# Where a mixture-of-experts stage issues its row gathers and weight fetches: ahead of a block's first layer, or behind it

## The chip, the cores and the metric

The kernel runs on one core of one Trainium2 chip. The metric is the device time of one execution in microseconds (us). The kernel before takes 1376.26 us as the median of 3 runs (1374.75 to 1378.42).

## What is computed

Three stages follow one another on 4608 tokens of width 512. Attention with keys and values pooled by eight gives `x`; a dense feed-forward layer with softplus replaces it; then comes the expert stage, which is where the change lies:

```
skip_score = x @ w_skip
do_compute = skip_score > 0
xc = x[do_compute]
logits = xc @ w_gate
e_idx = argmax(logits); gate_w = softmax(logits)[e_idx]
for e in range(8):
    h = max(xc[e_idx == e] @ w1[e], 0)
    y[e_idx == e] = gate_w * (h @ w2[e])
out[do_compute] = xc + y          (all other rows: out = x)
```

## The kernel before, in words

**Blocks.** The expert stage sorts the tokens by expert into blocks of up to 256 tokens (two halves, j = 0 and 1, of 128). A program of conditional blocks covers the worst case; block `i` is written by `superblock(i, ...)`. Blocks 0 to 9 form the first part (`NS1 = 10`), whose lists are made before the last group of tokens of the dense layer is ready; blocks 10 to 26 form the second part, nested in one another by conditions. Of these 27, the profiled execution runs 20, blocks 0 to 19; blocks past 19 are called dead here. Nothing is computed for a dead block, but a running block still issues the loads for the blocks that follow it, dead or not.

**One block.** TensorE (PE) does layer one in 96 matmuls (128x256, L898) into four PSUM tiles `h`. ScalarE (ACT) evicts each as `hh` (L902), VectorE (DVE) as the remainder `hl` (L903). Layer two is 24 matmuls (128x512, L922 to L924) for each half into `y`; DVE adds the residual (`ys`, L926) and GpSimd (POOL) scatters each half to `out` (L928). The second half is skipped when the block holds too few tokens.

**Loads, all issued by POOL on one queue.** `load_ids` (L349) fetches a block's row numbers, `gather` (L357) its rows by these numbers into `xg` (two DMAs, four buffers), `fetch` (L396) the weights of an expert into `raw1` (first layer) or `raw2` (second layer), one buffer of 2 MiB each. If a block has the same expert as the one before it, the fetch carries indices out of bounds and moves nothing. The list for `load_ids` of a dead block is out of bounds too, so a gather for one uses row numbers that an earlier block left.

**Weights into place.** When the expert changes, `split1` turns `raw1` into `w1h` (ACT, L405, four pieces) and `w1l` (DVE, L406, four pieces) behind layer one of the block before, under a condition (L911). `split2` does the same for the second layer (L413, L414) at the head of the block itself (L883).

**Rows into place.** `spread(i + 2)` at the head of block `i` transposes 32x32 pieces of `xg` on DVE (L380) and issues 16 DMAs on SyncE (SP, L385); `turn(i + 1)` in the middle of layer one writes the operands of the next block (L391, L392).

**What sets the order.** This stage is under a manual schedule: each engine runs its instructions in the order in which they are written. POOL's order in a block before the change is fetch `raw1` of the next block, gather for the block three ahead, row numbers for the block four ahead, fetch `raw2` of the next block, and then the two scatters:

```
            if more > 0:
                fetch("raw1", w1, i + 1)
            ...
            if more > 2:
                gather(i + 3)
            if more > 3:
                load_ids(i + 4)
            if i > 0 and i != NS1 - 1:
                with tc.If(changes(s)):
                    split2()
            if more > 0:
                fetch("raw2", w2, i + 1)
```

Of the kernel before, what the change touches and what calls it, by code (L numbers as in the profile page):

```python
# [36 lines left out]
def tile_kernel(ctx, tc, qT, kT, vT, wbits, w9, w1, w2, out):  # L37
# [7 lines left out]
    NS1 = 10  # L45
# [298 lines left out]
    def at(i):  # L344
        return (lists[1], i) if i < NS1 else (lists[2], i - NS1)

    def load_ids(i):
        li, s = at(i)
        nc.gpsimd.indirect_dma_start(  # L349
            out=ids[i % 5], out_offset=None, in_=tab,  # L350
            in_offset=bass.IndirectOffsetOnAxis(ap=li["tidx"][:, s:s + 1], axis=0),
            bounds_check=P * NCOL // 2 - 1, oob_is_err=False)

    def gather(i):
        rows = NTOK - G if i < NS1 else NTOK
        for j in range(2):
            nc.gpsimd.indirect_dma_start(  # L357
                out=xg[i % 4][j], out_offset=None, in_=x2d[:rows, :],
                in_offset=bass.IndirectOffsetOnAxis(ap=ids[i % 5][:, j:j + 1], axis=0),
                bounds_check=rows - 1, oob_is_err=False)  # L360
# [26 lines left out]
    def turn(i):  # L387
        xv = xm[i % 2].rearrange("p (q k j r) -> p j q k r", q=4, k=4, j=2)
        hv, lv = (t.rearrange("p k (j q r) -> p j q k r", j=2, q=4) for t in (xth[i % 2], xtl[i % 2]))
        for j in range(2):  # L390
            nc.scalar.activation(out=hv[:, j], in_=xv[:, j], func=AF.Copy)  # L391
            nc.vector.tensor_tensor(out=lv[:, j], in0=xv[:, j], in1=hv[:, j].bitcast(F32), op=ALU.subtract)  # L392

    def fetch(name, src, i):
        li, s = at(i)
        nc.gpsimd.indirect_dma_start(  # L396
            out=ws[name], out_offset=None, in_=src,
            in_offset=bass.IndirectOffsetOnAxis(ap=li["widx"][:, s:s + 1], axis=0),
            bounds_check=NE * P - 1, oob_is_err=False)

    def split1():
        raw = ws["raw1"].rearrange("p (a b) -> p a b", a=4)
        for q in range(4):
            cs = slice(q * 256, (q + 1) * 256)
            nc.scalar.activation(out=ws["w1h"][:, :, cs], in_=raw[:, :, cs], func=AF.Copy)  # L405
            nc.vector.tensor_tensor(out=ws["w1l"][:, :, cs], in0=raw[:, :, cs],  # L406
                                    in1=ws["w1h"][:, :, cs].bitcast(F32), op=ALU.subtract)

    def split2():
        raw = ws["raw2"].rearrange("p (a b) -> p a b", a=8)  # L410
        for q in range(4):
            cs = slice(q * 2, (q + 1) * 2)
            nc.scalar.activation(out=ws["w2h"][:, cs, :], in_=raw[:, cs, :], func=AF.Copy)  # L413
            nc.vector.tensor_tensor(out=ws["w2l"][:, cs, :], in0=raw[:, cs, :],  # L414
                                    in1=ws["w2h"][:, cs, :].bitcast(F32), op=ALU.subtract)
# [447 lines left out]
    def superblock(i, cond, mask, more, big=None):  # L863

        _, s = at(i)

        def changes(s_):
            return (mask & (1 << s_)) > 0

        with ExitStack() as st:  # L870
            if cond is not None:
                st.enter_context(tc.If(cond))
            if more > 0:
                fetch("raw1", w1, i + 1)
            if i == 0 and more > 0:
                gather(1)
                gather(2)
            if more > 2:
                gather(i + 3)
            if more > 3:  # L880
                load_ids(i + 4)
            if i > 0 and i != NS1 - 1:
                with tc.If(changes(s)):  # L883
                    split2()
            if more > 0:
                fetch("raw2", w2, i + 1)
            if more > 1 and i not in (0, NS1):
                spread(i + 2)
            xh, xl = xth[i % 2], xtl[i % 2]
            for fp in range(4):  # L890
                h = ps_f.tile([P, 2, SB], F32, tag="h", name="h")
                for f2 in range(2):
                    f0 = (fp * 2 + f2) * P
                    n = 0
                    for kk in range(4):
                        wh, wl = ws["w1h"][:, kk, f0:f0 + P], ws["w1l"][:, kk, f0:f0 + P]
                        for l, r in ((wh, xh), (wh, xl), (wl, xh)):
                            nc.tensor.matmul(h[:, f2, :], lhsT=l, rhs=r[:, kk, :],  # L898
                                             start=n == 0, stop=n == 11)
                            n += 1  # L900
                fs = slice(fp * 2, fp * 2 + 2)
                nc.scalar.activation(out=hh[:, fs, :], in_=h, func=AF.Relu)  # L902
                nc.vector.scalar_tensor_tensor(out=hl[:, fs, :], in0=h, scalar=0.0,  # L903
                                               in1=hh[:, fs, :].bitcast(F32),
                                               op0=ALU.max, op1=ALU.subtract)
                if fp == 1 and i > 0 and more > 0:
                    turn(i + 1)
            if more > 0:
                if i == 0:
                    flip(1, ps_t, "t")  # L910
                with tc.If(changes(s + 1)):  # L911
                    split1()
            if more > 1 and i in (0, NS1):
                spread(i + 2)
            for j in range(2):
                with ExitStack() as half:  # L916
                    if j and big is not None:
                        half.enter_context(tc.If((big & (32 << s)) > 0))
                    y = ps_o.tile([P, D], F32, tag=f"y{j}", name=f"y{j}")
                    js = slice(j * P, (j + 1) * P)  # L920
                    for f in range(8):
                        nc.tensor.matmul(y, lhsT=hh[:, f, js], rhs=ws["w2h"][:, f, :], start=f == 0, stop=False)  # L922
                        nc.tensor.matmul(y, lhsT=hh[:, f, js], rhs=ws["w2l"][:, f, :], start=False, stop=False)  # L923
                        nc.tensor.matmul(y, lhsT=hl[:, f, js], rhs=ws["w2h"][:, f, :], start=False, stop=f == 7)  # L924
                    r = xg[i % 4][j]
                    nc.vector.scalar_tensor_tensor(out=ys[j], in0=y, scalar=r[:, D:D + 1],  # L926
                                                   in1=r[:, :D], op0=ALU.mult, op1=ALU.add)
                nc.gpsimd.indirect_dma_start(  # L928
                    out=out, out_offset=bass.IndirectOffsetOnAxis(ap=ids[i % 5][:, j:j + 1], axis=0),
                    in_=ys[j], in_offset=None, bounds_check=NTOK - 1, oob_is_err=False)  # L930
# [84 lines left out]
```

## Time and profile before

| | |
|---|---|
| median of 3 runs | 1376.26 us (1374.75 to 1378.42) |
| time of the profiled execution | 1372.43 us |
| its span, first to last instruction | 1370.6 us |
| mean granted TensorE clock | 0.995 of full speed |
| PE busy | 1336.9 us, 98% of the span |
| DVE, ACT, POOL busy | 847.9, 594.5, 309.5 us |

The span leaves out 1.8 us of the profiled execution's own time, at its start and end. The expert stage's first layer-one matmul starts at 909.6 us, so the stage takes about 460 us. A time such as "1316.40" below is counted from the span's start. An engine is busy while it executes an instruction; the idle time ahead of an instruction is given in brackets with the event that ended it.

### The profile page before, as it was taken

The page shows a single profiled execution, that of the slowest core. Times are in us where ns is not written, and L with a number is a line of the kernel's source. Part 1 is how long each engine was busy: PE and PEld are TensorE (multiplying, and loading weights), DVE is VectorE, ACT ScalarE, POOL GpSimd, SP SyncE. Part 2 cuts the span into 40 slices and gives each one's busy share as a digit, 9 for nine tenths or more (in the row PEclk, how much of TensorE's full clock was granted, in tenths as well). Part 3 has the DMA queues.
Part 4 walks back from the last instruction along what each step waited for, and adds up shares of the span by engine and source line. Part 5 has one row for each costly group of instructions (what it writes and reads, how often), then busy time and mean ns, then how long its engine had stood idle before and what let it go on. Part 6 is the DMA issues. An engine that isn't in the chain of part 4 may idle for free. (4 is left out here: it accounts for less than half of the span.)

```text
span 1370.6 us, 21360 instructions
## 1 busy us (share of the span) xinstructions
PE 1336.9 (98%) x7030; PEld 1113.8 (81%) x7030; DVE 847.9 (62%) x1951; ACT 594.5 (43%) x1076; POOL 309.5 (23%) x374
## 2 busy tenths in 40 slices
PE   6999999999999999999999999999999999999986
PEld 5777887878878778778778878888989998889886
DVE  7997884974974965956947839534645432325254
ACT  6995554545445545545445445541111111114142
POOL 2010111121121030020120210342424243323332
PEclk9999999999999999999999999999999999999998
DMA  8643442241341340431411302513323122225272
GB/s 276 250 148 86 116 109 63 79 126 32 97 114 34 109 119 7 127 96 41 125 43 48 95 9 58 182 47 86 96 68 108 57 76 66 76 62 169 64 275 76
DMA packets 149600, 134.18 MB, mean 98 GB/s; under 512 B 100789, under 2 KB 116789, under 8 KB 146912
## 3 DMA queue, kind: packets, MB, share of 16 engines
q1 hardware_dynamic: 131744, 95.51, 24.1%
q0 software_dynamic: 17728, 37.13, 8.5%
q8 instruction: 60, 0.98, 0.3%
q14 instruction: 68, 0.56, 0.1%
HBM read 166.67 MB, written 29.67 MB: 143 GB/s over the span
## 5 line engine op out<-in xcount | busy, mean ns | idle before, releaser
L716 PE MATMUL h<-xh,wt 128*128 128x512 f32 x1152 | 379.6, 390 | 0.3 <-DVE xl L573 0.3
L716 PEld LDWEIGHTS h<-xh,wt 128*128 128x128 f32 x1152 | 216.2, 188 | 46.0 <-DVE xl L573 1.2
L898 PE MATMUL h<-xt,w1h 128*128 128x256 f32 x1280 | 229.2, 282 | 6.2 <-issue 2.8
L740 PE MATMUL y<-wt,gh 128*128 128x512 f32 x576 | 232.8, 404 | 0.0
L120 DVE CUSTOM_DVE_ANT_0 junk<-rows,w9b 128x512 bf16<-128x512 f32 x324 | 223.1, 689 | 8.1 <-ACT rows L114 3.2
L741 PE MATMUL y<-wt,gh 128*128 128x512 f32 x576 | 225.2, 391 | 0.0
L742 PE MATMUL y<-wt,gl 128*128 128x512 f32 x576 | 225.1, 391 | 0.0
L716 PE MATMUL h<-xl,wt 128*128 128x512 f32 x576 | 224.7, 390 | 0.0
L898 PEld LDWEIGHTS h<-xt,w1h 128*128 128x128 f32 x1280 | 197.9, 189 | 10.2 <-issue 5.6
L898 PE MATMUL h<-xt,w1l 128*128 128x256 f32 x640 | 180.3, 282 | 1.9 <-DVE w1l L406 0.8
L902 ACT ACTIVATE hs<-h 128x512 fp32r<-128x512 f32 x80 | 47.5, 597 | 310.5 <-PE h L898 159.2
L725 DVE SCALAR_TENSOR_TENSOR a<-h,a 128x512 f32<-128x512 f32 x144 | 98.8, 686 | 103.3 <-ACT a L724 102.5
L722 ACT ACTIVATE a<-h 128x512 f32<-128x512 f32 x144 | 85.8, 596 | 174.1 <-PE h L716 162.3
L727 ACT ACTIVATE gh<-a 128x512 fp32r<-128x512 f32 x144 | 91.0, 632 | 161.5 <-DVE a L725 159.7
L740 PEld LDWEIGHTS y<-wt,gh 128*128 128x128 f32 x576 | 108.2, 188 | 35.2 <-ACT a L722 7.3
L742 PEld LDWEIGHTS y<-wt,gl 128*128 128x128 f32 x576 | 108.1, 188 | 25.3 <-issue 2.1
L716 PEld LDWEIGHTS h<-xl,wt 128*128 128x128 f32 x576 | 108.2, 188 | 22.4 <-issue 0.2
L898 PEld LDWEIGHTS h<-xt,w1l 128*128 128x128 f32 x640 | 122.8, 192 | 2.5 <-DVE w1l L406 1.0
L741 PEld LDWEIGHTS y<-wt,gh 128*128 128x128 f32 x576 | 108.3, 188 | 20.0 <-issue 0.2
L729 DVE TENSOR_TENSOR gl<-a,gh 128x512 fp32r<-128x512 f32 x144 | 101.2, 702 | 37.4 <-ACT gh L727 34.0
L922 PE MATMUL y<-w2h,hs 128*128 128x512 f32 x304 | 119.1, 392 | 0.0
L924 PE MATMUL y<-w2h,hs 128*128 128x512 f32 x304 | 118.9, 391 | 0.0
(198 smaller groups left out, 1733.2 us busy)
## 6 DMA issues: line engine op xcount, KB each, us to landing
w9b<-w SPq DMA_DIRECT2D x81, 256.0 KB
raw<-wbits SPq DMA_DIRECT2D x12, 1024.0 KB
x2d<-rows SPq DMA_DIRECT2D x36, 260.0 KB
et<-q SPq DMA_DIRECT2D x256, 32.0 KB
kv<-vT SPq DMA_DIRECT2D x28, 288.0 KB
kv<-kT SPq DMA_DIRECT2D x24, 288.0 KB
xm<-misc SPq DMA_DIRECT2D x160, 32.0 KB
misc<-misc SPq DMA_DIRECT2D x144, 32.0 KB
```

The costliest lines, as they stand in the source:

```text
L120: nc.vector.tensor_tensor_reduce(out=ws["junk"], in0=rows[t][:, :D], in1=w9b[e], scale=1.0, scalar=0.0, op0=ALU.mult, op1=ALU.add, accum_o ...
L716: nc.tensor.matmul(h, lhsT=l, rhs=r[:, kk, :], start=n == 0, stop=n == 11)
L722: nc.scalar.activation(out=a, in_=h, func=AF.Abs)
L725: nc.vector.scalar_tensor_tensor(out=a, in0=h, scalar=0.0, in1=a, op0=ALU.max, op1=ALU.add)
L727: nc.scalar.activation(out=gh, in_=a, func=AF.Copy)
L729: nc.vector.tensor_tensor(out=gl, in0=a, in1=gh.bitcast(F32), op=ALU.subtract)
L740: nc.tensor.matmul(y, lhsT=th, rhs=wh, start=c == 0, stop=False)
L741: nc.tensor.matmul(y, lhsT=th, rhs=wl, start=False, stop=False)
L742: nc.tensor.matmul(y, lhsT=tl, rhs=wh, start=False, stop=c == 15)
L898: nc.tensor.matmul(h[:, f2, :], lhsT=l, rhs=r[:, kk, :], start=n == 0, stop=n == 11)
L922: nc.tensor.matmul(y, lhsT=hh[:, f, js], rhs=ws["w2h"][:, f, :], start=f == 0, stop=False)
L924: nc.tensor.matmul(y, lhsT=hl[:, f, js], rhs=ws["w2h"][:, f, :], start=False, stop=f == 7)
```

## The change

The fetch of `raw1` at the head of a block stays only in the first block of each part. In all blocks it is issued behind layer one and `split1`, and for the block after the next. The gather for the block three ahead and the row numbers for the block four ahead move from the head to the same place, behind that fetch.

```diff
-            if more > 0:
+            if i in (0, NS1) and more > 0:
                 fetch("raw1", w1, i + 1)
             if i == 0 and more > 0:
                 gather(1)
                 gather(2)
-            if more > 2:
-                gather(i + 3)
-            if more > 3:
-                load_ids(i + 4)
             if i > 0 and i != NS1 - 1:
                 with tc.If(changes(s)):
                     split2()
...
                     flip(1, ps_t, "t")
                 with tc.If(changes(s + 1)):
                     split1()
+            if more > 1:
+                fetch("raw1", w1, i + 2)
+            if more > 2:
+                gather(i + 3)
+            if more > 3:
+                load_ids(i + 4)
             if more > 1 and i in (0, NS1):
                 spread(i + 2)
```

POOL's rows of one block of the second part (block 17), from its first fetch to its first scatter. `raw1`, `raw2`, `xg`, `ids`, `ys0` and `ys1` are the names above; what a row waits for stands in brackets, where DMASW and a number is the landing of an earlier DMA of POOL. Before:

```order
L396 DMA raw1_8089<-w1,misc_8022 128x4096 [waits DMASW3_49,Activation_49]
L357 DMA xg0_8143<-x2d_73,ids0_123 128x520 [waits DMASW6_49]
L357 DMA xg0_8143<-x2d_73,ids0_123 128x520 [waits DMASW4_49]
L349 DMA ids1_124<-tab_74,misc_8022 128x2 [waits DMASW5_49,DMASW1_49]
L883 REGISTER_ALU
L883 COMPARE_AND_BRANCH
L883 UNCONDITIONAL_BRANCH x2
L396 DMA raw2_8139<-w2,misc_8022 128x4096 [waits DMASW7_49,DVE_49,Activation_49]
L911 REGISTER_ALU
L911 COMPARE_AND_BRANCH
L911 UNCONDITIONAL_BRANCH x2
L928 DMA out<-ys0_8497,ids2_125 4608x512 [waits DVE_49]
```

Now, from the same block's first fetch to its first scatter:

```order
L396 DMA raw2_8139<-w2,misc_8022 128x4096 [waits DMASW4_49,DVE_49,Activation_49]
L907 REGISTER_ALU
L907 COMPARE_AND_BRANCH
L907 UNCONDITIONAL_BRANCH x2
L396 DMA raw1_8089<-w1,misc_8022 128x4096 [waits DMASW5_49,DVE_49,Activation_49]
L357 DMA xg0_8143<-x2d_73,ids0_123 128x520 [waits DMASW0_49]
L357 DMA xg0_8143<-x2d_73,ids0_123 128x520 [waits DMASW6_49]
L349 DMA ids1_124<-tab_74,misc_8022 128x2 [waits DMASW7_49,DMASW2_49]
L930 DMA out<-ys0_8497,ids2_125 4608x512 [waits DVE_49]
```

The `raw2` fetch is now first, and the other four DMAs stand between `split1` (the condition of L907, which was L911) and the first scatter.

The end of the same block on POOL in the changed kernel, from the first scatter to the second:

```order
L930 DMA out<-ys0_8497,ids2_125 4608x512 [waits DVE_49]
L920 REGISTER_ALU
L918 COMPARE_AND_BRANCH
L918 UNCONDITIONAL_BRANCH x2
L930 DMA out<-ys1_8498,ids2_125 4608x512 [waits DMASW0_49,DVE_49]
```

These rows stand as they did, apart from their line numbers: in both kernels the second scatter waits for the landing of the first (the DMASW in its bracket is that of the first scatter).

DVE's rows of the same block in the changed kernel, from the end of the second layer's split to the first piece of the next block's `w1l`:

```order
L879 UNCONDITIONAL_BRANCH [waits DVE_49]
L380 STREAM_TRANSPOSE misc_8022<-xg3_8494 128x4x4x32 [waits DMAHW3_49,DMAHW4_49,DMAHW2_49,DMAHW5_49,DMAHW1_49,DMAHW6_49,DMAHW0_49,DMAHW7_49,DMASW6_49,DVE_49]
L380 STREAM_TRANSPOSE misc_8022<-xg3_8494 128x4x4x32 [waits DMASW7_49,DVE_49]
L899 SCALAR_TENSOR_TENSOR hs_8384<-h_13001,hs_8384 128x512 [waits Activation_49]
L899 SCALAR_TENSOR_TENSOR hs_8384<-h_13028,hs_8384 128x512 [waits Activation_49]
L392 TENSOR_TENSOR xt1_8383<-misc_8022,xt0_8382 128x4x4x32 [waits Activation_49] x2
L899 SCALAR_TENSOR_TENSOR hs_8384<-h_13059,hs_8384 128x512 [waits Activation_49]
L899 SCALAR_TENSOR_TENSOR hs_8384<-h_13086,hs_8384 128x512 [waits Activation_49]
L907 REGISTER_ALU
L907 COMPARE_AND_BRANCH
L406 TENSOR_TENSOR w1l_8186<-raw1_8089,w1h_8185 128x4x256 [waits DMASW5_49,Activation_49]
```

DVE's order is the same in both kernels. What differs is the gather that its transposes (L380) wait for: it was issued at the head of the block before, and now stands directly behind the `raw1` fetch at the end of the block before.

## Rows read from the trace of the kernel before

**Rows 1.** The page, busy time: engine, us (share of the span), instructions.

```profile
PE 1336.9 (98%) x7030; PEld 1113.8 (81%) x7030; DVE 847.9 (62%) x1951; ACT 594.5 (43%) x1076; POOL 309.5 (23%) x374
```

**Rows 2.** PE's waits, 900 to 1371 us: what waited, for what: total, times, longest.

```profile
PE h L898 <- ACT w1h L405: 1.5, 1, 1.5
...
PE h L898 <- PEq L916: 1.0, 1, 1.0
PE h L898 <- DVE w1l L406: 0.8, 1, 0.8
```

**Rows 3.** Line L405, ACT's pieces of `w1h`: count, ns min/median/max, first and last.

```profile
L405 ACT ACTIVATE w1h<-raw x16: 1042/1048/1057, 870.3 to 1336.7; 128x1024 fp32r<-128x1024 f32 x16
```

**Rows 4.** Timeline of PE, blocks 18, 19: start, us, instruction [idle before <- releaser].

```profile
1316.40 0.47 PE L898 MATMUL h<-xt,w1h 128*128 128x256 f32 x2 [0.98 <-PEq L916]
...
1328.25 0.39 PE L924 MATMUL y<-w2h,hs 128*128 128x512 f32 x1
...
1334.94 0.50 PE L898 MATMUL h<-xt,w1h 128*128 128x256 f32 x2 [1.53 <-ACT w1h L405]
...
1349.10 0.50 PE L924 MATMUL y<-w2h,hs 128*128 128x512 f32 x1
```

**Rows 5.** Busy time by stretch: layer one of 18, of 19, slow stretch (PEclk third last).

```profile
1316.40:1327.80 11.40, 11.40 (x97) 11.40 (x98) 9.01 (x12) 6.51 (x9) 6.73 (x5) 1.00 0.30 85
1334.94:1348.59 13.65, 12.89 (x97) 12.69 (x97) 11.24 (x12) 9.19 (x12) 5.07 (x4) 0.87 0.39 144
1336.80:1340.00 3.20, 3.20 (x17) 3.20 (x17) 3.20 (x4) 0.93 (x1) 0.00 (x0) 0.50 0.86 320
```

**Rows 6.** Timeline of ACT: block 18's last eviction, block 19's splits.

```profile
1328.20 0.60 ACT L902 ACTIVATE hs<-h 128x512 fp32r<-128x512 f32 x1 [2.40 <-DVE hs L903]
1333.83 3.90 ACT L405 ACTIVATE w1h<-raw 128x1024 fp32r<-128x1024 f32 x4 [5.04 <-DMA raw<-w,misc]
1341.52 3.91 ACT L413 ACTIVATE w2h<-raw 128x1024 fp32r<-128x1024 f32 x4 [3.79 <-issue]
```

**Rows 7.** Timeline of DVE, blocks 16 to 19.

```profile
1288.03 0.69 DVE L903 SCALAR_TENSOR_TENSOR hs<-h,hs 128x512 fp32r<-128x512 f32 x1 [0.43 <-ACTq L911]
...
1299.62 1.30 DVE L380 STREAM_TRANSPOSE misc<-xg 128x512 f32<-128x512 f32 x2 [0.62 <-DVEq L883]
...
1311.63 4.63 DVE L406 TENSOR_TENSOR w1l<-raw,w1h 128x1024 fp32r<-128x1024 f32 x4 [0.26 <-ACT w1h L405]
...
1323.85 1.30 DVE L380 STREAM_TRANSPOSE misc<-xg 128x512 f32<-128x512 f32 x2
...
1348.39 1.25 DVE L903 SCALAR_TENSOR_TENSOR hs<-h,hs 128x512 fp32r<-128x512 f32 x2
...
1350.76 1.29 DVE L903 SCALAR_TENSOR_TENSOR hs<-h,hs 128x512 fp32r<-128x512 f32 x2
```

**Rows 8.** Timeline of POOL, blocks 17 to 19.

```profile
1321.18 1.36 POOL L928 DMA_INDIRECT out<-ys,ids  x1 [2.95 <-DVE w2l L414]
1322.85 2.01 POOL L396 DMA_INDIRECT raw<-w,misc  x1 [0.31 <-ACT hs L902]
1325.16 1.01 POOL L357 DMA_INDIRECT xg<-x2d,ids  x1 [0.31 <-DVE misc L380]
...
1329.41 1.00 POOL L396 DMA_INDIRECT raw<-w,misc  x1 [0.30 <-issue]
...
1361.10 1.00 POOL L928 DMA_INDIRECT out<-ys,ids  x1 [4.62 <-DVE ys L926]
```

**Rows 9.** Chain of waits that ended last: start, us, what: first scatters of 18, 19.

```profile
1340.49 2.40 DMA out<-ys,ids
...
1355.46 4.85 DMA out<-ys,ids
```

**Rows 10.** Timeline of SP's DMA issues, blocks 18 and 19.

```profile
1325.24 16.10 SPq L385 DMA_DIRECT2D misc<-misc  x16
1348.56 10.45 SPq L385 DMA_DIRECT2D xm<-misc  x16
```

## The prediction

> **What bounds the kernel now.** I read the page's busy times first, then PE's waits in the expert stage, then the timelines of the engines where such a wait is longest. PE is busy for 98% of the span [rows 1], so a load that is issued elsewhere can give time back only where PE waits for it. The list of PE's waits shows how little that is: in 460 us it waited 1.5 us for ACT's `w1h`, 0.8 us for DVE's `w1l` and 1.0 us for its own sequencer behind a skipped half block [rows 2]. The pieces of `w1h` number 16, four for each new expert [rows 3]; four of them are the initial load, so only three blocks change the expert. Their timelines show them to be 15, 18 and 19. All other `raw1` fetches move nothing.
>
> Both weight waits belong to the last change, into block 19. PE starts that block at 1334.94 after 1.53 us of idling [rows 4], and the 0.8 us for `w1l` [rows 2] follow directly. ACT shows why: it starts the split of block 19 at 1333.83 after 5.04 us of waiting for the `raw1` fetch [rows 6], which POOL issued at 1322.85 [rows 8], 11.0 us earlier. Blocks 17 and 18 both skip their second half, so two changes of expert follow one another with little work between them. [...]
>
> The profiled execution took 1372.43 us, 3.8 us below the median of 1376.26. I work out differences against the trace and add them to the median; a difference of 0.3%, 4.1 us, is about what a measurement of this kernel can tell from none.
>
> **The change, part by part.** *Blocks without a new expert.* There the moved DMAs hide. DVE ends layer one's last eviction in block 16 at 1288.72 and needs gathered rows at 1299.62 [rows 7], 10.9 us later; POOL's four steps at some 1.3 us each [rows 8] take 5.2 of these. The cover is layer two. The first scatter goes out about a microsecond late, and nobody waits for it before the second one. I cost these blocks at nothing. Were the gather late, DVE's transposes would wait, and behind them the evictions that layer two reads.
>
> *The `raw1` fetch of block 19.* It now waits for `split1` of block 18, which ends on DVE at 1316.26 (1311.63 and 4.63) [rows 7], instead of going out at 1322.85. With the 11.0 us that it took before it lands at about 1327.4. ACT's last eviction in block 18 ended at 1328.80 [rows 6], so the split starts some 5 us earlier than before. On PE this is worth at most 2.8 us: layer one would start 0.98 us after block 18's layer two, as block 18 did behind a skipped half, in place of 1.53 us [rows 4], which gives 0.55; and it would take 11.40 in place of 13.65 us [rows 5], which gives 2.25.
>
> *What is late next: the second layer's weights.* Layer two of block 19 can't start without `hl`. DVE makes that only after `split2` and the transposes: ACT starts `split2` at 1341.52 [rows 6], and the first `hl` is ready at about 1349.08 (1348.39 and a little over half of the 1.25 us that two of them take) [rows 7], 7.56 us later. PE's third matmul of layer two, the first to read `hl`, started at 1349.10 [rows 4]. So DVE set that moment already before the change, and PE's 2.8 us are worth nothing unless `split2` starts earlier too. That depends on the `raw2` fetch, issued at 1329.41 [rows 8], 12.1 us before `split2`. In the new order POOL issues `raw1`, two gathers and row numbers from 1316.4, which took 6.56 us from 1322.85 to 1329.41 [rows 8], so the first scatter of block 17 goes out at 1323.0. If the queue is served in order, it lands behind 2 MiB of `raw1`, at 1328.5 or so; the second scatter waits for that, the `raw2` fetch is issued 1.67 us after it (1321.18 to 1322.85) [rows 8], at 1330.8, and with 11.0 us `split2` starts at 1341.8. That is +0.3 us against before. [...] I take +0.3, since the two fetches of block 19 took 11.0 and 12.1 us [rows 6, 8].
>
> *The tail.* In block 19 POOL now issues four DMAs for dead blocks after layer one, before its first scatter. DVE's last `hl` ends at 1352.05 [rows 7]; 0.35 us later POOL starts, and 5.2 us later, at 1357.6, it reaches the first scatter, which went out at 1355.46 [rows 9]: 2.1 us late. The second scatter, the kernel's last work, waits for the first to land. It went out at 1361.10 [rows 8], 0.8 us after a landing that took 4.85 us [rows 9]; block 18's, with fewer rows, took 2.40. With 2.40 the second would go out as before (DVE's `ys` sets it then), with 4.85 it is 2.1 us late. I take the middle, a landing of 3.6 us and +0.9, because SP's transfers, which shared the DMA engines with the first scatter until 1359.0 (1348.56 and 10.45) [rows 10], are nearly over by then, while two gathers stand ahead of it.
>
> *Sum.* 0.3 and 0.9 make +1.2 us: 1373.6 for a profiled execution like this one, **1377.5** against the median.
>
> [...] The rows say 11.0 us for a fetch of 2 MiB [rows 6, 8]. [...] But the fetch in that row shared the DMA engines with SP's transfers from 1325.24 on [rows 10], and in the new order `raw1` goes out nine microseconds ahead of them.
>
> **Rivals.**
>
> [...]
>
> *Second, slower: the gather behind the weights holds DVE.* In block 18 DVE's transposes, which ran at 1323.85 [rows 7], now wait for a gather that was issued behind `raw1`. If that lands at 1327.4 and the gathers of 0.26 MB each follow in turn, at about 1 us each, the second is there at 1329.3 and the first `hl` of block 18 at 1330.7. Layer two of block 18, whose third matmul was due at 1328.25 [rows 4], stalls for 2.4 us. The same queue makes the first scatter late, `raw2` goes out at 1332.4 and lands 12.1 us later at 1344.5: `split2` 3.0 us late. With the tail's 2.1 the sum is +5.1, 1381.4. The point from which it decides is where the gather lands later than 1327 (in my forecast it does by a little, and the stall is paid out of the 2.8 us that PE would have had to wait later anyway). For it: one queue, and DVE's fixed order. Against it: the slack just named.
>
> *Third: the earlier fetch isn't earlier.* The `raw1` fetch waits for DVE and ACT to pass L911; if that releases it only after DVE's next work, at 1321 or later, block 19 starts as before, and only the tail changes: 1376.3 to 1378.4. The result reads the same as my forecast.
>
> **Chances.** My forecast, with the third rival, 0.62: 1376 to 1379. The first rival 0.25, around 1374. The second 0.13, around 1381. The first one's 2.8 us lie inside 0.3%, so faster by over 0.3% needs something I don't see or a shift of the median: 0.05. Slower by over 0.3% comes from the second rival, most of it: 0.12. Within 0.3%: 0.83. The range runs from the first rival's end, 1373.5, up to 1381.0, just short of the second's centre.
>
> **What would show it.** Right: PE's wait for `w1h` and `w1l` at the start of block 19 is gone and the clock stays at 1.00 there; ACT's start of `split2` in block 19 stays at about 25.1 us after the start of layer one of block 18 (1316.40 to 1341.52); the last block's scatters leave closer together, with the first of them later. [...] A difference above 6 us in either direction, or one that lies in blocks 0 to 16, would mean that I misread where the stage's waits are.

## The result, and the profile after

The changed kernel takes **1361.98 us** (median of 5 runs, 1360.46 to 1363.2) against 1376.26 for the kernel before; the ratio is 0.9894, with a 95% interval of 0.9881 to 0.9908. That is 14.3 us faster, outside the range of the prediction (1373.5 to 1381.0). The profiled execution took 1360.56 us, 11.9 less than the one of before, with a span of 1358.8.

Where the 11.9 us lie is read by blocks. Busy time by stretch, kernel before, from the first layer-one matmul of block 0 to that of block 18 (after the stretch and its length stand PE, PEld, DVE, ACT, POOL, the granted clock, DMA share, GB/s):

```profile
909.61:1316.40 406.79, 400.25 (x2586) 363.96 (x2587) 167.99 (x338) 73.23 (x121) 145.25 (x142) 1.00 0.32 95
```

The same view of the changed kernel, from block 0 to block 18, block 18, and block 19 up to the last scatter's issue:

```profile
908.84:1305.81 396.97, 395.32 (x2586) 361.77 (x2587) 168.00 (x338) 74.69 (x122) 138.92 (x139) 1.00 0.32 96
1305.81:1323.87 18.06, 17.04 (x120) 15.66 (x121) 13.47 (x17) 10.33 (x14) 8.55 (x7) 1.00 0.61 217
1323.87:1349.35 25.48, 22.75 (x144) 20.13 (x144) 12.91 (x17) 7.00 (x10) 14.17 (x13) 1.00 0.42 124
```

Blocks 0 to 17 give 406.79 - 396.97 = **9.82 us**. Block 18 gives 0.48 (it took 18.54 from 1316.40 to 1334.94 [rows 4]), block 19 up to its last scatter 0.68 (26.16, from 1334.94 to 1361.10 [rows 4, 8]), and the stage began 0.77 us earlier. So the prediction argued about a tenth of the difference, that of blocks 18 and 19. Five sixths lie in blocks in which, but for block 15, no weights change; of these 9.82 us block 0 alone has 3.95 (26.83 against 22.88 us).

The same 2586 matmuls fill 400.25 us before and 395.32 after; the rest of the 9.82 us is idle time of PE, 6.54 against 1.65. Of the 4.93 us in busy time, 1.4 are TensorE's clock: behind a layer one in which PE idled for 1.83 us, the granted clock of block 0 of the kernel before is 0.50 for 3.4 us:

```profile
923.60:927.00 3.40, 3.20 (x9) 2.62 (x9) 2.48 (x4) 2.07 (x4) 0.00 (x0) 0.50 0.01 2
```

Its layer two takes 12.41 us; in the changed kernel, where the clock stays at 1.00, it takes 11.00. PE's waits from 905 to 1320 us, kernel before (what waited, for what, total us, times, longest):

```profile
PE h L898 <- issue: 3.3, 9, 0.7
PE tr L368 <- issue: 1.3, 2, 0.9
PE h L898 <- PEq L916: 1.0, 1, 1.0
...
```

The same list of the changed kernel, complete:

```profile
PE h L894 <- PEq L918: 1.0, 1, 1.0
PE h L894 <- ACT rows L114: 0.7, 1, 0.7
PE h L894 <- DVEq L962: 0.7, 1, 0.7
```

The rows put down to "issue", waits for nothing that the profile shows, are gone. By their total, 3.3 us, they stand at the top of the list that gave [rows 2], and the prediction passed over them. Block 12 of the kernel before shows what they belong to. It begins at 1184.08. First ACT's timeline:

```profile
1187.16 0.60 ACT L902 ACTIVATE hs<-h 128x512 fp32r<-128x512 f32 x1 [13.16 <-DVE misc L380]
1194.17 0.60 ACT L902 ACTIVATE hs<-h 128x512 fp32r<-128x512 f32 x1 [6.41 <-PE h L898]
```

POOL's, in the same block:

```profile
1185.32 1.00 POOL L928 DMA_INDIRECT out<-ys,ids  x1 [4.41 <-DVEq L883]
1186.62 1.05 POOL L396 DMA_INDIRECT raw<-w,misc  x1 [0.30 <-issue]
1187.97 1.01 POOL L357 DMA_INDIRECT xg<-x2d,ids  x1 [0.31 <-issue]
1189.29 1.01 POOL L357 DMA_INDIRECT xg<-x2d,ids  x1 [0.30 <-issue]
1190.60 1.00 POOL L349 DMA_INDIRECT ids<-tab,misc  x1 [0.30 <-issue]
1191.90 0.99 POOL L396 DMA_INDIRECT raw<-w,misc  x1 [0.30 <-issue]
```

PE's: the matmul that ends the second quarter of layer one, and the one row with idle time:

```profile
1189.62 0.28 PE L898 MATMUL h<-xt,w1l 128*128 128x256 f32 x1
...
1194.10 0.39 PE L898 MATMUL h<-xt,w1h 128*128 128x256 f32 x2 [0.66 <-issue]
```

ACT's second eviction waits for the second quarter of layer one, which is due 5.65 us into the block at the 11.31 us that an undisturbed layer one takes. It starts 10.09 us in, 1.3 us after the end of POOL's last DMA. The profile names PE as what it waited for, and the trace shows what was late: the matmul that ends the quarter started on time, at 1189.62, but its signal (the step of the semaphore that ACT waits for) is recorded only at 1194.09, 4.5 us later. PE's matmuls meanwhile start without a gap, and then PE pauses too, in the middle of its last quarter, where the program has no wait. I call this the **hold-up**. In the changed kernel only the `raw2` fetch is left at the head. ACT in its block 12, which begins at 1176.99:

```profile
1180.07 0.60 ACT L898 ACTIVATE hs<-h 128x512 fp32r<-128x512 f32 x1 [13.11 <-DVE misc L380]
1182.90 0.60 ACT L898 ACTIVATE hs<-h 128x512 fp32r<-128x512 f32 x1 [2.23 <-PE h L894]
```

POOL there:

```profile
1178.22 1.00 POOL L930 DMA_INDIRECT out<-ys,ids  x1 [3.42 <-DVEq L879]
1179.53 1.04 POOL L396 DMA_INDIRECT raw<-w,misc  x1 [0.30 <-DVE misc L380]
1190.74 1.02 POOL L396 DMA_INDIRECT raw<-w,misc  x1 [10.17 <-DVEq L907]
```

The second eviction starts 5.91 us in; the matmul before it started at 1182.52, and its signal came 0.3 us later. Block by block, layer one took 14.42 us in block 0 before and 11.88 after; in block 1, 12.20 and 11.31; in blocks 11 to 14, 16 and 17, 11.76 to 12.36 and 11.31; in blocks 2 to 9 the two are equal. Evictions are late in blocks 2 to 7 as well (in block 3 the third starts 10.14 us in, and 8.73 in the changed kernel), but there PE loses nothing by it.

So two questions stood: which of POOL's DMAs at the head causes the hold-up, and by what.

### The profile page after: what moved, and what is told of

Same layout as the page of the kernel before. It is cut to its first block, busy times and chain, and to the rows that moved or that the text cites. A ratio compares the mean times of both kernels' runs of the same rounds, so it can differ in the third digit from the quotient of the medians.

```text
span 1358.8 us, 21365 instructions
## 1 busy us (share of the span) xinstructions
PE 1330.1 (98%) x7030; PEld 1110.0 (82%) x7030; DVE 847.6 (62%) x1951; ACT 595.0 (44%) x1076; POOL 308.0 (23%) x375
## 5 line engine op out<-in xcount | busy, mean ns | idle before, releaser
L894 PE MATMUL h<-xt,w1h 128*128 128x256 f32 x1280 | 226.4, 281 | 2.7 <-PEq L918 2.0
L928 DVE SCALAR_TENSOR_TENSOR ys<-y,xg 128x512 f32<-128x512 f32 x38 | 28.5, 750 | 145.3 <-PE y L926 115.8
L926 PE MATMUL y<-w2h,hs 128*128 128x512 f32 x304 | 118.5, 390 | 0.6 <-DVE hs L899 0.6
```

What stands on the lines that cost most here:

```text
L894: nc.tensor.matmul(h[:, f2, :], lhsT=l, rhs=r[:, kk, :], start=n == 0, stop=n == 11)
```

## The experiments

The runs fall into seven sessions, each on one chip with the kernel before beside it. This mattered more than expected: in two of the sessions the kernel before took 1363 us, and one of these two chips gave 1371 in another session. The table names for twelve of the profiles the session, the time of blocks 0 to 17, when ACT's second eviction starts in blocks 11 to 14, and how many landings of DMAs the trace recorded in all.

| kernel | session (median of before) | blocks 0 to 17 | 2nd eviction, us in | landings recorded |
|---|---|---|---|---|
| before | 1 (1376.26) | 406.79 | 7.1 to 10.1 | 14,859 |
| changed | 1 | 396.97 | 5.9 | 14,419 |
| rows only | 2 (1375.52) | 407.8 | 9.0 to 10.4 | 14,797 |
| three empty at the head | 3 (1376.87) | 403.73 | 7.8 to 9.0 | 13,793 |
| two loads at the head | 3 | 397.26 | 5.9 | 14,756 |
| three empty behind | 4 (1363.01) | 396.88 | 5.9 | 18,457 |
| before, again | 5 (1370.59) | 406.0 | 7.7 to 10.0 | 14,808 |
| changed, again | 5 | 396.88 | 5.9 | 14,549 |
| three empty at the head, again | 5 | 400.18 | 7.4 to 8.7 | 13,889 |
| three empty behind, again | 5 | 405.75 | 5.9 to 6.5 | 13,821 |
| changed, timed | 6 (1362.75) | 397.35 | 5.9 | 17,742 |
| before, profiled | 7 (1374.02) | 409.44 | 9.0 to 10.5 | 14,719 |

### The two halves of the change

*Rows only:* the kernel before with the gathers and row numbers behind layer one, the `raw1` fetch left at the head.

```diff
-            if more > 2:
-                gather(i + 3)
-            if more > 3:
-                load_ids(i + 4)
...
                     split1()
+            if more > 2:
+                gather(i + 3)
+            if more > 3:
+                load_ids(i + 4)
```

> The kernel before with only the gathers and the row numbers moved behind layer one; raw1 is fetched at the head, one block ahead, as before. Theory T (the gathers' transfers, beside others in flight during layer one, made the engines stop for nothing that the profile names): layer one of blocks 0 and 1 and 11 to 17 comes down to 11.3 to 11.9 us, blocks 0 to 17 together lose about 9.8 us of their 406.8, block 19 still waits for w1h and w1l, and the profiled execution is 1362 to 1364. Rival W (it is the first-layer fetch at the head that costs): layer one of these blocks stays at 12.0 to 12.4 and the time within 1 us of before.

Measured: 1369.52 us, ratio 0.9951 (0.9935 to 0.9967). Neither expectation holds: the loss in blocks 0 to 17 is all there, and yet the time falls by 6 us. POOL's timeline in block 12 (which begins at 1183.45) says why:

```profile
1185.99 1.04 POOL L396 DMA_INDIRECT raw<-w,misc  x1 [0.30 <-DVE misc L380]
1187.34 1.01 POOL L396 DMA_INDIRECT raw<-w,misc  x1 [0.31 <-ACT hs L898]
1188.65 1.01 POOL L357 DMA_INDIRECT xg<-x2d,ids  x1 [0.30 <-issue]
1189.97 1.01 POOL L357 DMA_INDIRECT xg<-x2d,ids  x1 [0.30 <-issue]
1191.28 1.00 POOL L349 DMA_INDIRECT ids<-tab,misc  x1 [0.30 <-issue]
```

The gathers are written behind layer one, but POOL has nothing to wait for there and issues them at once, each 0.30 us after the DMA ahead of it. What moves them in the changed kernel is the wait of the `raw1` fetch ahead of them, for ACT and DVE. What this run gains it gains in blocks 18 and 19 (17.66 and 22.03 us up to PE's last matmul, against 18.54 and 24.89), where the `raw2` fetch is now the second DMA and no longer the fifth.

*First-layer weights only:* the `raw1` fetch moves, gathers and row numbers stay.

```diff
-            if more > 0:
+            if i in (0, NS1) and more > 0:
                 fetch("raw1", w1, i + 1)
...
                     split1()
+            if more > 1:
+                fetch("raw1", w1, i + 2)
```

> The kernel before with only the raw1 fetch moved, two blocks ahead and behind layer one; gathers and row numbers stay at the head. Theory T: blocks 0 to 17 stay at 406 to 407 us; only block 19 changes, its waits for w1h and w1l go, and the profiled execution is 1370 to 1372. Rival W: blocks 0 to 17 lose about 9.8 us and it is 1361 to 1363.

Measured: 1371.31 us, ratio 0.9965 (0.995 to 0.998). Blocks 0 to 17 take 403.32, which is neither expectation: one DMA fewer at the head takes away about a third of the loss. In blocks 12, 13 and 16 the second eviction starts 8.8 to 9.0 us in and layer one takes its 11.31 us all the same; a delay of 3 us costs PE nothing there. Block 19 gets worse (30.68 us up to PE's last matmul).

### Transfers, or the issuing of them

*A load at the head:* the changed kernel with a plain load of 512 KB by POOL.

```diff
+            if more > 2:
+                nc.gpsimd.dma_start(out=dum, in_=w1[0:P, 0:1024])
             if i > 0 and i != NS1 - 1:
```

> The changed kernel with one plain load of 512 KB (128 rows of 4 KB of w1, into a tile that nobody reads), issued by POOL at the head of each block that gathers. Theory T in its plain form (any half megabyte there does it): layer one of blocks 11 to 14, 16 and 17 goes back up by 0.4 to 1 us each, 3 to 6 us in all. Rival P (it is how many DMAs POOL issues in a row at the head, or the gathers' small pieces, not the bytes): less than 1 us in all.

Measured: 1365.03 us, ratio to before 0.9917 (0.9892 to 0.9943); blocks 0 to 17 in 396.94, evictions on time. Bytes of that size do nothing to layer one.

*The pieces of SP moved:* the kernel before with `spread` behind layer one in all blocks.

```diff
-            if more > 1 and i not in (0, NS1):
-                spread(i + 2)
...
-            if more > 1 and i in (0, NS1):
+            if more > 1:
                 spread(i + 2)
```

> The kernel before with the spread (DVE's transposes and SP's 16 DMAs) behind layer one in all blocks, the gathers at the head as before. If the loss needs the gathers and SP's transfers together: layer one of blocks 11 to 17 comes down to 11.3 us, blocks 0 and 1 stay, 4 to 5 us less in all, unless ACT waits for rows that now arrive later. If the gathers alone do it: blocks 11 to 17 stay at 11.8 to 12.4.

Measured: 1387.64 us, ratio 1.008 (1.0053 to 1.0107). In block 12, which begins at 1186.62, SP issues nothing between 1189.91 and 1202.84, and layer one still takes 13.0 us; in blocks 11 to 17, but for 15, it takes 12.5 to 13.1. A collision with SP is not needed. Why it takes longer than in the kernel before is not shown.

### One, two, three more indirect DMAs at the head

All three start from the changed kernel. *Row numbers at the head* and *gathers at the head* put one part back:

```diff
+            if more > 3:
+                load_ids(i + 4)
             if i > 0 and i != NS1 - 1:
```

> The changed kernel with the row numbers alone back at the head, ahead of the raw2 fetch; gathers and raw1 stay behind layer one. The measure is when ACT starts the second eviction of layer one in blocks 11 to 17: 5.9 us after the block's first matmul in the changed kernel, 7.0 to 10.1 us before. Theory G (the gathers' own transfers) and theory B (any half megabyte or more in flight when the eviction is due): stays at 5.9. Theory N (POOL issuing three or more DMAs in a row beside layer one): at most 0.5 later.

```diff
+            if more > 2:
+                gather(i + 3)
             if i > 0 and i != NS1 - 1:
```

> The changed kernel with the gathers alone back at the head, ahead of the raw2 fetch; row numbers and raw1 stay behind layer one. Theories G, B and N all: ACT's second eviction in blocks 11 to 17 starts 1 us or more later than 5.9 us after the block's first matmul; PE loses 0 to 0.4 us in each. If it stays at 5.9, the gathers by themselves are not the cause.

Measured: 1366.68 us with the row numbers, blocks 0 to 17 in 398.07, the second eviction on time; 1366.58 us with the gathers, 399.33, the second eviction at 7.4 to 7.8 us.

*Three empty ones* adds three indirect DMAs whose index is that of the unchanged expert, out of bounds, so that they move nothing in blocks that keep their expert:

```diff
+            if more > 2:
+                li, s3 = at(i + 1)
+                for j in range(3):
+                    nc.gpsimd.indirect_dma_start(
+                        out=dumi[j], out_offset=None, in_=tab,
+                        in_offset=bass.IndirectOffsetOnAxis(ap=li["widx"][:, s3:s3 + 1], axis=0),
+                        bounds_check=NE * P - 1, oob_is_err=False)
             if i > 0 and i != NS1 - 1:
```

> The changed kernel with three more indirect DMAs of POOL at the head whose indices are out of bounds, so that they move nothing (except in the blocks with a new expert). Theory N: ACT's second eviction in blocks 11 to 17 starts at 7 us or later, and PE loses some tenths. Theories G and B: it stays at 5.9.

*Two loads* adds two plain ones of 512 KB in the same place:

```diff
+            if more > 2:
+                for j in range(2):
+                    nc.gpsimd.dma_start(out=dum[j], in_=w1[0:P, j * 1024:(j + 1) * 1024])
             if i > 0 and i != NS1 - 1:
```

> The changed kernel with two plain loads of 512 KB in 4 KB rows, issued by POOL at the head, into tiles that nobody reads: 1 MB in flight from 3.5 to about 8.5 us after the block's first matmul, across the moment of 5.9 us at which the second eviction is due. Theory B: ACT's second eviction in blocks 11 to 17 starts at 7 us or later. Theories G and N: it stays at 5.9 to 6.1.

Measured: 1371.9 us with three empty DMAs, 1361.35 with two loads of half a megabyte. Block 12 of the run with the empty ones begins at 1182.02; ACT:

```profile
1185.10 0.60 ACT L906 ACTIVATE hs<-h 128x512 fp32r<-128x512 f32 x1 [13.11 <-PE h L902]
1191.04 0.60 ACT L906 ACTIVATE hs<-h 128x512 fp32r<-128x512 f32 x1 [5.34 <-PE h L902]
```

and POOL, the last of the empty ones and the `raw2` fetch:

```profile
1187.22 1.00 POOL L882 DMA_INDIRECT dumi<-tab,misc  x1 [0.30 <-issue]
1188.53 1.00 POOL L396 DMA_INDIRECT raw<-w,misc  x1 [0.30 <-issue]
```

In the run with the two loads block 12 begins at 1177.35. ACT:

```profile
1183.26 0.60 ACT L902 ACTIVATE hs<-h 128x512 fp32r<-128x512 f32 x1 [2.23 <-PE h L898]
```

and POOL:

```profile
1179.57 1.19 POOL L881 DMA_DIRECT2D dum<-w  x2
1181.06 1.07 POOL L396 DMA_INDIRECT raw<-w,misc  x1 [0.30 <-ACT hs L902]
```

So half a megabyte or a whole one in flight doesn't count; a row of indirect DMAs does, even where none of them moves a byte. Whether plain DMAs in such a row would do the same, this run can't say: POOL's last DMA at the head ends 4.78 us into the block, before the eviction is due. That POOL is issuing at the moment is not enough: with the row numbers at the head its last indirect DMA ends 6.6 us in, later than with the gathers (6.2), and nothing is late in block 12. Counted at the head of block 12, not counting the scatter: one or two give 5.9 us, three 7.4, four 8.8 (weights only) and 9.0 (the empty ones), five 10.1 to 10.2. In the kernel before, with rows only and with the empty ones, ACT resumes 1.3 to 1.5 us after the end of POOL's last. In the four runs of this section block 19 is slower than in the changed kernel as well; that says nothing on the hold-up of the other blocks.

### Three runs in a session without the hold-up

Meant to tell place, kind and mere busyness of POOL apart, again from the changed kernel: the three empty DMAs behind the row numbers; three plain loads of 1 KB at the head; three memsets at the head.

```diff
                 load_ids(i + 4)
+            if more > 2:
+                li, s3 = at(i + 1)
+                for j in range(3):
+                    nc.gpsimd.indirect_dma_start(
...
```

> The changed kernel with the three empty indirect DMAs of the run before last, now behind a block's first layer (after the row numbers), in place of its head. Theory N (a run of indirect DMAs on GpSimd beside layer one holds ACT, DVE and PE up; beside layer two it costs nothing): blocks 0 to 17 take 397 to 399 us, ACT's second eviction of blocks 11 to 17 starts 5.9 us into the block; what the later scatter costs in blocks 18 and 19 is 2 to 4 us; 1362 to 1366 us. Rival P (what counts is how many indirect DMAs a block has, wherever they stand): blocks 0 to 17 take 403 to 404 us as with the three at the head, 1371 us.

```diff
+            if more > 2:
+                for j in range(3):
+                    nc.gpsimd.dma_start(out=dumi[j], in_=tab[0:P, :])
             if i > 0 and i != NS1 - 1:
```

> The changed kernel with three plain loads of 1 KB each by GpSimd at the head of a block, where the run with three empty indirect DMAs had those. Theory N-indirect (only indirect DMAs, whose descriptors follow from a table of rows, hold the engines up): blocks 0 to 17 take 397 us, ACT's second eviction on time at 5.9 us; about 1361 to 1362 us. Rival N-any (any run of four DMAs issued by GpSimd does it): blocks 0 to 17 take 403 to 404 us, the second eviction of blocks 11 to 13 at 8 to 9 us, about 1370 us.

```diff
+            if more > 2:
+                for j in range(3):
+                    nc.gpsimd.memset(dum, 0.0)
             if i > 0 and i != NS1 - 1:
```

> The changed kernel with three memsets of 128x1040 on GpSimd at the head of a block (about 1.0 us each in the trace, as long as an indirect DMA). Theory N (it is the DMAs): blocks 0 to 17 take 397 us, the second eviction at 5.9 us, 1361 to 1362 us. Rival M (any stretch of 4 to 5 us in which GpSimd is busy beside layer one holds the others up, as by a shared way to memory): blocks 0 to 17 take 400 to 404 us and the second eviction starts at 7 to 9 us, 1366 to 1371 us.

Measured: 1366.23, 1362.33 and 1366.21 us; blocks 0 to 17 in 396.88, 396.88 and 397.26, with every second eviction on time; what the first and the third lose against the changed kernel they lose in blocks 18 and 19. That looks like a clean win for the theory of the indirect DMAs, and it is none: in session 4 the kernel before took **1363.01 us**. Nothing was held up there, so that these runs can't tell what holds up. Plain loads of 1 KB and memsets were not run again, and stay open.

### The same kernels in one later session, on the same chip

> The kernel before, unchanged, with a profile on this chip. If the hold-up belongs to the program: about 1376 us, blocks 0 to 17 take 406 to 408 us, ACT's second eviction of blocks 11 to 17 at 7 to 10 us. If it belongs to a chip or a moment: 1362 to 1364 us in some sessions, blocks 0 to 17 then take 397 us and the second eviction starts at 5.9 us; then only blocks 18 and 19 differ from the changed kernel.

> The changed kernel, unchanged: 1360.5 to 1363 us and blocks 0 to 17 in 397 us by either theory.

> The changed kernel with three empty indirect DMAs at the head of a block, as run before. If the hold-up belongs to the program: blocks 0 to 17 take 402 to 405 us, 1370 to 1373 us. If to a chip or a moment: as the kernel before on this chip, 397 us for blocks 0 to 17 where that one is not held up.

> The changed kernel with the three empty indirect DMAs behind the first layer, as run before. Theory N, on a chip where the kernel before is held up: blocks 0 to 17 take 397 to 399 us. Rival P (their number in a block counts, not their place): 402 to 404 us. On a chip where the kernel before is not held up it tells nothing.

Measured, with nothing edited: the kernel before 1371.23 us, the changed one 1361.17, three empty at the head 1368.85 (blocks 0 to 17 in 400.18, a little under what was expected), three empty behind layer one 1376.48. The hold-up is back, on the same chip, and the change is worth 9.1 us in blocks 0 to 17 (406.0 and 396.88). The last of the four is the telling one, because the identical kernel had been profiled without it. PE's waits from 905 to 1305 us in the earlier session:

```profile
PE h L895 <- ACT rows L114: 0.7, 1, 0.7
PE h L895 <- DVEq L970: 0.7, 1, 0.7
```

and in this one:

```profile
PE h L895 <- issue: 3.4, 8, 0.8
PE y L934 <- DVE hs L900: 2.9, 3, 1.4
PE h L895 <- ACT rows L114: 0.7, 1, 0.7
PE h L895 <- DVEq L970: 0.7, 1, 0.7
...
```

Both theories of that run miss. Layer one of blocks 12 to 15 and 17 takes its 11.31 us, as the theory of the place says; that of blocks 1 to 7, 11 and 16 takes 11.40 to 12.40. In block 4 this is easy to follow. The run of eight DMAs ahead of it (fetch, gathers, row numbers, empty ones, scatter) ends only in its layer one: the block begins at 1003.81, POOL's last of them ends at 1007.23, and ACT's first eviction starts at 1009.08, 5.3 us in and not 3.1. So behind layer one is no safe place as such. The changed kernel's run of five there is over before the next block begins; one of eight isn't. Where the run ends isn't all, though: in blocks 11, 12 and 16 it ends 1.6 to 1.7 us in, and layer one takes 11.67, 11.31 and 12.21 us.

### What separates the two kinds of session

> The changed kernel, timed in rounds with the kernel before. In a session with the hold-up: before 1370 to 1377 us, the changed kernel 1361 to 1362 us, ratio 0.989 to 0.994. In a session without it: before 1362 to 1364 us, the changed kernel 1360.5 to 1362.5 us, ratio 0.998 to 1.000; by the prediction's own sum, were it right there, 1.001.

Measured: the changed kernel 1361.93 us beside 1362.75 for the kernel before, **ratio 0.9994 (0.9985 to 1.0004)**. A second session without the hold-up, on another chip; the change is worth nothing that can be measured there.

> The kernel before, unchanged, with a profile. In a session without the hold-up (1361 to 1365 us): blocks 0 to 17 take 397 to 398 us, layer one of blocks 11 to 17 takes 11.31 us, ACT's second eviction starts 5.9 us into the block, the page has no idle time of PE put down to issue above 1 us, and the record holds some 17,700 landings. In one with it (1370 to 1377 us): 406 us, 12 us, 7 to 10 us, some 14,800 landings.

Measured: 1373.64 us, with the hold-up: 409.44 us in blocks 0 to 17. None of the profiles of the kernel before is without it.

The table's last column separates the two kinds. Where nothing is held up the trace holds 17,700 to 18,600 landings of DMAs, and where the kernel before is held up it holds 13,800 to 15,300, in every profile of each kind. That goes for the changed kernel too (14,419 and 14,549 against 17,742), whose time is the same in both kinds (1361.17 to 1361.98 us): missing records alone cost nothing that can be measured. What is missing is missing in the expert stage: of the kernel with three empty DMAs behind layer one, 1,650 to 1,770 landings in each of four stretches of 100 us in one session, 710 to 990 in the other; in the nine stretches before the stage it is 480 to 1,390 against 430 to 1,340. The records of the transfers themselves are as many in both, 151,390.

### A version on top

Row numbers between the two scatters, in the changed kernel.

```diff
-            if more > 3:
-                load_ids(i + 4)
...
                     in_=ys[j], in_offset=None, bounds_check=NTOK - 1, oob_is_err=False)
+                if j == 0 and more > 3:
+                    load_ids(i + 4)
```

> The changed kernel with the row numbers issued between the two scatters in place of ahead of them. Theory (the tail and the first scatter of blocks 18 and 19 are late by GpSimd's four steps, and the second scatter waits for the first to land, so one step fits between them): the first scatter goes out 1.3 us earlier in each block, PE's wait of 0.6 us in layer two of block 19 is gone or shorter, the last scatter goes out 0.5 to 1.3 us earlier in the block; blocks 0 to 17 as in the changed kernel (397 us); 0.5 to 2 us faster than it, about 1360.5 us, ratio to before 0.988. Rival (the first scatter waits for DVE's rows anyway, or the second is set by the step between them): same as the changed kernel within 0.5 us, or slower by up to 1.

Measured, in session 4: 1360.48 us (11 runs), ratio to the kernel before in that session 0.9982 (0.9973 to 0.9991). POOL's two last scatters (layer two of block 19 begins at 1334.86):

```profile
1344.42 1.03 POOL L928 DMA_INDIRECT out<-ys,ids  x1 [0.30 <-issue]
1348.81 1.02 POOL L928 DMA_INDIRECT out<-ys,ids  x1 [2.02 <-DVE ys L926]
```

They go out 9.6 and 13.9 us into layer two, against 10.3 and 14.1 in the changed kernel. PE's wait for `hl` in layer two of block 19 did not get shorter (1.25 us, 0.57 in the changed kernel). It is the fastest median of all, but it never ran beside the changed kernel: 0.9982 and 0.9994, each against the kernel before in its own session, have intervals that overlap. Its blocks 0 to 17 take 396.96 us, as the changed kernel's.

## Why the prediction was wrong

**The step that failed** is the one on blocks without a new expert: "I cost these blocks at nothing." It priced what the moved DMAs cost where they go, and that part held but for the size of one term. It never priced what they cost where they stood. Four indirect DMAs ahead of the `raw2` fetch at the head cost 9.8 us in blocks 0 to 17, in sessions like the one of the comparison (the changed kernel, without them there, has none of it); PE's signals come late beside them, in block 12 by 4.5 us after the matmul's start in place of 0.3.

**What led to it** was the sentence that 98% of busy PE leaves time only where PE waits for loads. Half of the 9.82 us lay inside the busy time (400.25 against 395.32 us for 2586 matmuls), and the visible waits were filed under "issue". The row that speaks against that sentence was in the list that the prediction read, at its top, and ACT's idle rows of 6 us in the middle of layer one were in the trace. No term of the prediction's sum stands for these blocks. Its last sentence named the sign, "one that lies in blocks 0 to 16", and that is what happened.

**The `raw1` fetch of block 19** came out as said. Rows of the changed kernel, PE:

```profile
1323.87 0.47 PE L894 MATMUL h<-xt,w1h 128*128 128x256 f32 x2 [1.02 <-PEq L918]
1336.45 0.50 PE L926 MATMUL y<-w2h,hs 128*128 128x512 f32 x1 [0.57 <-DVE hs L899]
```

ACT, the splits for block 19:

```profile
1317.94 3.90 ACT L405 ACTIVATE w1h<-raw 128x1024 fp32r<-128x1024 f32 x4
1328.63 3.91 ACT L413 ACTIVATE w2h<-raw 128x1024 fp32r<-128x1024 f32 x4 [6.80 <-DMA raw<-w,misc]
```

and POOL: `raw1` for block 19, the second scatter of block 17, `raw2` for block 19, and then that block's two scatters:

```profile
1306.49 1.01 POOL L396 DMA_INDIRECT raw<-w,misc  x1 [12.64 <-ACT w2h L413]
...
1317.57 1.00 POOL L930 DMA_INDIRECT out<-ys,ids  x1 [3.67 <-DVE hs L899]
1318.87 1.36 POOL L396 DMA_INDIRECT raw<-w,misc  x1 [0.30 <-issue]
...
1345.55 1.03 POOL L930 DMA_INDIRECT out<-ys,ids  x1 [0.30 <-issue]
1349.35 1.00 POOL L930 DMA_INDIRECT out<-ys,ids  x1 [2.76 <-DVE ys L928]
```

PE starts block 19 after 1.02 us of its own sequencer (predicted 0.98), layer one takes 1335.25 - 1323.87 = 11.38 us in place of 13.65, and the granted clock stays at 1.00, where it was 0.87 [rows 5].

**What is late next** was mis-sized. `split2` starts 22.8 us after block 18's layer one (1305.81 to 1328.63), where the prediction said 25.4. Three terms make the difference: the second scatter of block 17 goes out 11.8 us into block 18 (said 12.7), the fetch follows 1.30 us later (said 1.67), and it takes 9.8 us (said 11.0). The mechanism held: DVE's `hl` still ends last, and PE waits 0.57 us for it. But the term that was put at +0.3 us came out as -2.3 (22.8 us for the 25.1 of before), and PE reaches the third matmul of layer two of block 19 30.6 us after block 18's start (1305.81 to 1336.45) in place of 32.7 (1316.40 to 1349.10), and so keeps 2.1 of the 2.8 us that the prediction gave up. The lower end of the range, 1373.5, and the first rival's place in the chances stand on a fetch of 2 MiB in some 7 us. No run shows that term: the `raw2` fetch took 9.8 us here, and the fetches of block 19 took 11.0 and 12.1 before [rows 6, 8]. What that rival has PE keep, 2.8 us, came true in part, by these 2.1.

**The second rival** was right in its first half. In block 18 DVE's transposes wait for the gather behind the weights:

```profile
1315.57 1.37 DVE L380 STREAM_TRANSPOSE misc<-xg 128x512 f32<-128x512 f32 x2 [4.06 <-issue]
```

That it was the gather follows from the program's order; the profile names no releaser. PE was not stalled by it: layer two of block 18 took 5.7 us up to its last matmul, and 5.6 before.

**The tail** is right in sign and about right in size. The first scatter goes out 10.3 us into layer two of block 19 (1335.25 to 1345.55), 3.4 us later than before (1348.59 to 1355.46, 6.9), the last one 14.1 against 12.5: 1.6 us, of which PE's 0.57 is one part. The prediction said 0.9.

**As a forecast for the sessions without the hold-up** the prediction would have been near: "within 0.3%" holds there (0.9994), its own centre of +1.2 us (1.0009) lies just above the interval (0.9985 to 1.0004). That is no support for its costing of the blocks: it holds only where moving these DMAs gains nothing.

**What stays open** is by what means POOL's indirect DMAs make PE's signals late, and why only in some sessions. Shown is that the number of indirect DMAs matters (ACT's second eviction in block 12 starts 5.9 us in with one or two of them at the head, 10.1 to 10.2 with five), and so does their place (in one session blocks 0 to 17 took 400.18 us with three empty ones at the head, 405.75 with them behind layer one); that bytes don't (396.94 us with half a megabyte at the head, 397.26 with a whole one); that the hold-up needs no transfers of SP (layer one of block 12 took 13.0 us without them); and that it goes with a trace that lacks a fifth to a quarter of its landings (13,800 to 15,300 against 17,700 to 18,600). Whether plain DMAs or other work on POOL, as long and as close together, would do the same is not shown. Nor is a run of such DMAs beside layer one always harmful: in block 18 of the changed kernel POOL issues five in a row from 1306.49 us on, and ACT's evictions there are on time, the second 5.98 us in. One explanation would fit the sessions, and is the author's guess alone: the hold-up may be a cost of recording the execution, and a kernel slower for being watched. No run here shows that: every time here comes with a recorded execution.

## What to carry to other kernels

Price a moved step twice: what it costs where it goes, and what it cost where it stood. An engine's late start in the middle of a stage and idle time put down to "issue" are a price to ask after, even at 98% busy. And a step without a wait of its own is not moved by being written later (the gathers of *rows only* still went out 5.2 us into block 12, in the middle of layer one); the step ahead of it that waits is what moves it. Measure kernels that are compared in the same session, and look at the kernel before in each: three runs here looked conclusive until its time beside them was read.

## What the runs showed of the hardware that was not expected

- Beside indirect DMAs that POOL issued one behind the other, PE's signals came late, and with them the evictions on ACT and DVE: in the kernel before, the matmul that ends the second quarter of block 12 signalled 4.5 us after its start in place of 0.3 in the changed kernel. PE then paused for 0.66 us without a wait that the profile names. It happened even where the DMAs move nothing: in one session blocks 0 to 17 took 403.73 us with three empty ones at the head, and 397.26 with two plain loads of 512 KB there, where POOL's last DMA at the head ends 4.78 us into block 12, before the eviction is due.
- The same program on the same chip gave 1363.0 us in one session and 1370.6 to 1371.2 in another, at mean granted clocks of 0.994 to 0.998 and of 0.996 to 0.997. The traces of the two kinds differ by a fifth to a quarter in the landings that they hold (13,800 to 15,300 against 17,700 to 18,600).
- PE's busy time holds part of a hold-up: 4.9 of 9.8 us were in matmuls that the profile counts as busy, 1.4 of them at a granted clock of 0.50 behind 1.83 us of idling.
